# Keys', features' and q's float32 products moved to halves of TensorE's columns or rows

## The chip, the cores and the metric

One core of a Trainium2 chip runs one program. The metric is the device time of one execution in microseconds (us). TensorE is PE in the views, and its weight loads are PEld; VectorE is DVE, ScalarE is ACT, GpSimd is POOL, and SyncE (SP) issues the DMAs.

## What is computed

Linear attention with a product feature map, 4 batches, 4 heads, 1088 tokens, head width 32, r = 8, followed by a gated MLP (d_model 128, d_ff 1024) over the joined heads:

```python
def phi(x):
    a = np.einsum('rd,bhsd->bhsr', S1, x)
    b = np.einsum('rd,bhsd->bhsr', S2, x)
    return np.einsum('bhsi,bhsj->bhsij', a, b).reshape(*x.shape[:-1], r * r)
q_p, k_p = (phi(q), phi(k))
kv = np.einsum('bhsf,bhsd->bhfd', k_p, v)
z = np.sum(k_p, axis=2)
num = np.einsum('bhsf,bhfd->bhsd', q_p, kv)
den = np.einsum('bhsf,bhf->bhs', q_p, z)[..., None] + 1e-06
x = num / den                       # then [batch, seq, 128]
h = gelu(x @ w_in); u, v = halves of h
v_n = layernorm(v) * g_ln
v_s = np.einsum('ts,bsd->btd', w_sg, v_n) + b_sg[None, :, None]
out = x + (u * v_s) @ w_out
```

## The kernel before

Tokens are padded to 9 tiles of 128. Most of the work is the token-mixing product with `w_sg` (tiles `w_h`, `w_l` against the split features `ar`, PSUM tiles `pz`, lines 844 to 846). There, and in the products with `w_in` and `w_out`, a float32 number is split into a high and a low `float32r` word, and three matmuls (high x high, low x high, high x low) take the place of one float32 matmul.

Attention of a batch stands before that. For batches 1 to 3 it is written in `attention(b)`:

- **k step** (`k1`, L938): per token tile, one plain float32 matmul of the keys (128 columns of weights) with `sk` (128 moving columns, of which 64 are zero) gives both factors of the feature map. ACT copies one factor (L941), and DVE multiplies the two to 256 features (`features`, L260).
- **kv step** (`k2`, L951): per token tile, two float32 matmuls, one for each pair of heads; weights are 128 feature columns, 128 columns of v and ones move. Nine tiles add up in one PSUM tile.
- **q step** (`q2`, L975 to L980): per block `ci` of 364 tokens, q is split into two `float32r` words (ACT L969, DVE L970), and two matmuls (batches 2 and 3) or three (batch 1) of 364 columns give the factors. They go to DRAM (`dq`) and come back spread over partitions (`ea`, `eb`), are multiplied, split and used in `q3` (L1007 to L1009).

Batch 0 has its own code at the start: `k1_0` (L525), `k2_0` (L529), and `q2_0` (L603 to L605: 12 triples of 384 columns, from words that ACT and POOL make first). Before it, 14 small matmuls on a 64-column weight tile (L255) run; 12 more (`keep`, L707) stand where the main work is not ready yet.

Every step is a task with an engine; the list `ORDER` gives the sequence of all 1970 tasks, and each engine issues its own in that order. PSUM has three tiles `ps` for all steps of attention and of the MLP's inner products; a task that takes one waits until its last user has freed it.

Of the kernel before, what the change touches and what calls it, by code (L numbers as in the profile page):

```python
# [18 lines left out]
P = 128  # L19
NT = 9  # L20
# [125 lines left out]
class Plan:  # L146
# [9 lines left out]
    def add(self, eng, dur, f, r=(), w=(), take=(), free=(), pos=None, after=(), order=(), dma=(), port=0, tune=None):  # L156
# [13 lines left out]
        for k in r:  # L170
            if k not in w:
                self.read.setdefault(k, []).append(n)
        deps.discard(n)
        self.tasks.append(dict(eng=eng, dur=dur, f=f, deps=deps, take=take, free=list(free), pos=pos, order=set(order) - deps, dma=dma, port=port))
        return n

    def run(self):
# [1203 lines left out]
```

## Time and profile before

| | |
|---|---|
| median of 3 runs | 330.86 us (330.86 to 330.93) |
| span of the profiled execution | 328.9 us, so some 2.0 us of a run's time lie around the span |
| PE busy | 324.7 us, 99% of the span |
| DVE, ACT, POOL busy | 82%, 68%, 16% |
| chain that ended last | PE 99% |

The profiled execution has no time of its own beside its span; the 2.0 us are the median less the span. PE's records are durations from issue to a modelled end, and neighbours overlap. What one matmul costs in a full stream is the distance from one start to the next. A plain float32 matmul leaves two records.

### The profile page before, as it was taken

The numbers are of one execution on the slowest core, as the hardware profiler recorded it, in microseconds if no ns is written. First come the engines' busy times: TensorE is split into PE (matmuls) and PEld (weight loads), VectorE is DVE, ScalarE is ACT, GpSimd is POOL, SyncE is SP. The second block draws the span as 40 slices with busy tenths as digits, with TensorE's granted clock in tenths as the row PEclk, the third lists the DMA queues.
The fourth block names the chain that finished last, engine by engine and source line by source line (L and its number), as shares of the span: only waits on it lengthen the run. The fifth ranks groups of instructions, "written<-read, shape, count | busy, mean of one in ns | idle before, by whom it ended". The sixth has DMA issues, their size and how long they took to land.

```text
span 328.9 us, 5899 instructions
## 1 busy us (share of the span) xinstructions
PE 324.7 (99%) x1994; PEld 312.9 (95%) x1994; DVE 268.5 (82%) x595; ACT 223.3 (68%) x533; POOL 53.5 (16%) x130
## 2 busy tenths in 40 slices
PE   8999999999999999999999999999999999999996
PEld 8998899999999999999999999999999999999995
DVE  4799979999986899999883779897974587886755
ACT  6759994679899787457898776547889843522421
POOL 2696781000004200000013200000002200000000
PEclk9999999999999999999999999999999999999999
DMA  7999264675667777964675035932381029116702
GB/s 236 358 399 315 77 206 145 182 202 150 195 174 229 240 180 212 300 234 113 182 245 176 3 104 162 326 106 86 84 296 41 2 67 289 65 68 192 229 0 70
DMA packets 43854, 57.06 MB, mean 173 GB/s; under 512 B 4208, under 2 KB 41136, under 8 KB 43824
## 3 DMA queue, kind: packets, MB, share of 16 engines
q1 hardware_dynamic: 43680, 56.62, 54.8%
q8 instruction: 15, 0.25, 0.3%
q14 instruction: 15, 0.12, 0.1%
q10 hardware_dynamic: 144, 0.06, 0.1%
HBM read 46.73 MB, written 9.95 MB: 172 GB/s over the span
## 4 chain that ended last, share of the span: by engine, by line
PE 99%; DVE 0%; issue 0%; POOL 0%; POOLq 0%
PE pz L844 16%; PE pz L845 16%; PE pz L846 15%; PE ps L951 4%; PE ps L759 2%; PE ps L760 2%; PE po L798 2%; PE ps L761 2%; PE po L796 2%; PE po L797 2%; PE pz L855 2%; PE pz L856 2%; PE ps L938 2%; PE ps L1040 2%; PE ps L1041 2%; PE ps L1042 2%
## 5 line engine op out<-in xcount | busy, mean ns | idle before, releaser
L844 PE MATMUL pz<-w_h,ar 128*128 128x420 f32 (+1 forms) x288 | 94.4, 328 | 0.0
L845 PE MATMUL pz<-w_h,ar 128*128 128x420 f32 (+1 forms) x288 | 93.2, 324 | 0.0
L846 PE MATMUL pz<-w_l,ar 128*128 128x420 f32 (+1 forms) x288 | 93.1, 323 | 0.0
L844 PEld LDWEIGHTS pz<-w_h,ar 128*128 128x128 f32 x288 | 54.2, 188 | 1.9 <-DVE gt L775 0.4
L845 PEld LDWEIGHTS pz<-w_h,ar 128*128 128x128 f32 x288 | 54.1, 188 | 1.0
L846 PEld LDWEIGHTS pz<-w_l,ar 128*128 128x128 f32 x288 | 54.2, 188 | 0.6
L819 ACT CAST ar<-vn 128x512 fp32r<-128x512 f32 x40 | 24.5, 618 | 20.8 <-PE pz L846 19.9
L765 ACT ACTIVATE u<-ps 128x420 f32<-128x420 f32 (+1 forms) x48 | 22.4, 470 | 14.3 <-DVE gt L789 9.4
L790 ACT CAST gh<-gt 128x420 fp32r<-128x420 f32 (+1 forms) x47 | 23.0, 494 | 12.8 <-DVE gt L789 9.7
L820 DVE TENSOR_TENSOR ar<-vn,ar 128x512 fp32r<-128x512 f32 x40 | 27.2, 679 | 2.4 <-ACT ar L819 2.1
L323 ACT ACTIVATE vn<-vn,st 128x512 f32<-128x512 f32 x33 | 26.0, 811 | 1.4 <-POOL st L317 0.9
L791 DVE TENSOR_TENSOR gl<-gt,gh 128x420 fp32r<-128x420 f32 (+1 forms) x47 | 24.7, 531 | 1.6 <-ACT gh L790 1.2
L789 DVE TENSOR_TENSOR gt<-gt,u 128x420 f32<-128x420 f32 (+1 forms) x47 | 24.7, 532 | 0.5
L775 DVE SCALAR_TENSOR_TENSOR gt<-pz,g_col,b_bc 128x420 f32<-128x420 f32 (+1 forms) x31 | 17.8, 575 | 5.9 <-PE pz L856 3.8
L713 POOL TENSOR_TENSOR w_l<-w_f,w_h 128x420 fp32r<-128x420 f32 (+1 forms) x21 | 21.5, 1051 | 3.1 <-ACT w_h L666 2.7
L1052 ACT ACTIVATE kp<-vn,st 128x512 bf16<-128x512 f32 x27 | 19.4, 719 | 0.4
L1049 ACT ACTIVATE vn<-ps 128x512 f32<-128x512 f32 x27 | 16.0, 592 | 3.2 <-PE ps L1042 3.1
L306 POOL TENSOR_TENSOR st<-st 128x4 f32<-128x4 f32 (+2 forms) x8 | 2.2, 281 | 95.0 <-DVE st L288 95.0
L759 PE MATMUL ps<-x_h,win_h 128*128 128x420 f32 (+1 forms) x48 | 15.9, 332 | 0.0
L760 PE MATMUL ps<-x_h,win_l 128*128 128x420 f32 (+1 forms) x48 | 15.8, 329 | 0.0
L796 PE MATMUL po<-gh,wout_h 128*128 128x420 f32 (+1 forms) x47 | 15.7, 335 | 0.0
L761 PE MATMUL ps<-x_l,win_h 128*128 128x420 f32 (+1 forms) x48 | 15.7, 327 | 0.0
(311 smaller groups left out, 821.8 us busy)
## 6 DMA issues: line engine op xcount, KB each, us to landing
w_l<-td SPq DMA_DIRECT2D x52, 210.0 KB
w_h<-td SPq DMA_DIRECT2D x26, 420.0 KB
td<-tmp SPq DMA_DIRECT2D x16, 315.0 KB
w_f<-in_w SPq DMA_DIRECT2D x9, 544.0 KB
eb<-dq SPq DMA_DIRECT2D x12, 182.0 KB
ea<-dq SPq DMA_DIRECT2D x12, 182.0 KB
vn<-in_k SPq DMA_DIRECT2D x3, 576.0 KB
tmp<-in_w SPq DMA_DIRECT2D x16, 105.0 KB
```

Of the source, the lines that this page charges most:

```text
L323: A.activation(self.vn(t), self.vn(t), AF.Identity, bias=self.nm[:, t : t + 1], scale=self.rs[:, t : t + 1])
L759: mm(o, lhsT=win_h[:, ws], rhs=xh[:, cs], start=True, stop=False)
L760: mm(o, lhsT=win_l[:, ws], rhs=xh[:, cs], start=False, stop=False)
L765: add("A", 0.02 + ap(cw), lambda: A.activation(utt[plan.got[u]][:, :cw], ps(k)[:, :cw], AF.Gelu_apprx_tanh), r=[k], take={u: "u"}, free=[k ...
L789: add("V", dv(cw), lambda: V.tensor_mul(gt(k)[:, :cw], gt(k)[:, :cw], utt[plan.got[u]][:, :cw]), r=[u], w=[k], free=[u], port=1)
L790: add("A", ac(cw), lambda: A.copy(ght[plan.got[h]][:, :cw], gt(k)[:, :cw]), r=[k], take={h: "gh"})
L791: add("V", dv(cw), lambda: V.tensor_sub(glt[plan.got[l]][:, :cw], gt(k)[:, :cw], f32(ght[plan.got[h]][:, :cw])), r=[h, k], take={l: "gl"}, ...
L819: add("A", ac(n), lambda: A.copy(dst[:, 0], q()), r=r, w=[key])
L820: add("V", dv(n), lambda: V.tensor_sub(dst[:, 1], q(), f32(dst[:, 0])), r=r, w=[key], port=1)
L844: mm(o, lhsT=ar[e][:, 0, t], rhs=wh, start=first, stop=False, skip_group_check=True)
L845: mm(o, lhsT=ar[e][:, 1, t], rhs=wh, start=False, stop=False, skip_group_check=True)
L846: mm(o, lhsT=ar[e][:, 0, t], rhs=wl, start=False, stop=last, skip_group_check=True)
```

## The change

- k step: each token tile's 128 tokens are split in two halves of 64. Each half is a matmul with 64 columns of weights and 64 moving columns (`sk[:, :64]`); the first writes PSUM partitions 0 to 63, the second 64 to 127. In batches 2 and 3 three tiles make one task with one ACT copy; in batch 1 a task remains one tile.
- kv step: one matmul per head (64 weight columns, 64 moving columns), written to the two halves of the partitions in turn. In batches 2 and 3 all nine tiles are one task; the features now lie in `vn` instead of three turning `kp` tiles.
- q step: no split into words. Two plain float32 matmuls, each with the same 64 weight columns and one half (182 columns) of the block, on the two halves of the columns. The store to `dq` is two DMAs, the `eb` fill one DMA instead of two, the `ea` fill two as before.
- batch 0 likewise: `k1_0` 18 half products, `k2_0` 36, and `q2_0` 12 float32 products of 384 columns with 64 rows of weights each, in place of 36 `float32r` ones.
- The feature columns are ordered by head, the mask and `kv` are made to fit; the words `sk_h`, `sk_l`, `sk_w` and `qt` are gone. `ORDER` is new throughout; `free` now also waits for a tile's last readers when the list is made, and some helpers return their instruction. Nothing else changes.

```diff
-    step("skh", "A", 0.27, lambda: A.copy(sk_h, sk), ["sk"])
-    step("skl", "V", 0.25, lambda: V.tensor_sub(sk_l, sk, f32(sk_h)), ["skh"], w=["sk_l"], port=1)
...
     def k1_0(c):
-        for t in range(3 * c, 3 * c + 3):
-            mm(ps(("pk0", c))[:, P * (t % 3) : P * (t % 3) + P], lhsT=k0[:, P * t : P * t + P], rhs=sk, start=True, stop=True)
...
+        for i in range(6):
+            t, e = 3 * c + i // 2, i % 2
             mm(
+                ps(("pk0", c))[64 * e : 64 * e + 64, 64 * (i // 2) : 64 * (i // 2) + 64],
+                lhsT=k0[:, P * t + 64 * e : P * t + 64 * e + 64], rhs=sk[:, :64], start=True, stop=True,
+            )
+
+    def by_head(o, t, kp, v0, v1):
+        for h in range(H):
+            p, e, d = h // 2, 64 * (h % 2), D * (h % 2)
+            mm(
+                o[e : e + 64, 64 * p : 64 * p + 64], lhsT=kp[:, 64 * h : 64 * h + 64], rhs=(v1 if p else v0)[:, :, d : d + D],
                 start=(t == 0 and p == 0), stop=(t == NT - 1 and p == 1), skip_group_check=True,
             )
...
-    def q2_0(j, i):
-        o, s2 = pab0(j, i), [x[:, P * (2 * i + j % 2) :][:, :P] for x in sw]
-        h, l = qw[j // 2]
-        mm(o, lhsT=s2[0], rhs=h, start=True, stop=False)
-        mm(o, lhsT=s2[0], rhs=l, start=False, stop=False)
-        mm(o, lhsT=s2[1], rhs=h, start=False, stop=True)
+    def q2_0(c, i):
+        for p in range(2):
+            r = slice(64 * p, 64 * p + 64)
+            mm(pab0(2 * c + p, i), lhsT=sab()[r, i, p], rhs=q0[c][r], start=True, stop=True)
...
+        size = 1 if b == 1 else 3
+        for c in range(NT // size):
+            pk = ("pk", b, c)
+
+            def k1(c=c, pk=pk):
+                for i in range(2 * size):
+                    t, e = size * c + i // 2, i % 2
                     mm(
-                        ps(pkv)[:, P * p : P * p + P], lhsT=kpt(t % 3)[:, P * p : P * p + P],
-                        rhs=vh(1)[:, 0 : t + 2 : t + 1] if p else vh(0)[:, t : NT + 1 : NT - t],
-                        start=(t == 0 and p == 0), stop=(t == NT - 1 and p == 1), skip_group_check=True,
+                        ps(pk)[64 * e : 64 * e + 64, 64 * (i // 2) : 64 * (i // 2) + 64],
+                        lhsT=vn[:, t, 256 * s + 64 * e : 256 * s + 64 * e + 64], rhs=sk[:, :64], start=True, stop=True,
                     )
...
+        def k2(ts):
+            for t in ts:
+                by_head(ps(pkv), t, vn[:, t, 256 * s : 256 * s + 2 * P], vh(0)[:, t : NT + 1 : NT - t], vh(1)[:, 0 : t + 2 : t + 1])
+
+        for ts in [range(t, t + 1) for t in range(NT)] if b == 1 else [range(NT)]:
...
-            add("A", ac(cw), lambda cw=cw: A.copy(qtt[0][:, :cw], qld[:, :cw]), r=["qld"], w=["qh"])
...
+            def q2(hw=hw, pab=pab):
+                for e in range(2):
+                    mm(ps(pab)[64 * e : 64 * e + 64, :hw], lhsT=sk[:, 64:], rhs=qld[:, hw * e : hw * e + hw], start=True, stop=True)
...
+            add("A", ap(hw), lambda hw=hw, pab=pab: A.copy(abt[:, :hw], ps(pab)[:, :hw]), r=[pab], w=["ab"], free=[pab])
```

**PE at the start** (batch 0; L534 is `k1_0`, L611 `q2_0`, L542 `k2_0` of the change, L525, L603 to L605 and L529 those of before). Before:

```order
L525 MATMUL ps_118<-sk,k_99 128x128 x3
L525 MATMUL ps_119<-sk,k_99 128x128 x3
L529 MATMUL pz_121<-sg_vx,vn 128x128 x8
L603 MATMUL po_122<-ar_91,ar_93 128x384
L604 MATMUL po_122<-ar_92,ar_93 128x384
L605 MATMUL po_122<-ar_91,ar_94 128x384
```

The change:

```order
L534 MATMUL ps_113<-sk,k_95 64x64 x6
L611 MATMUL po_117<-r_97,sg_sab 128x384
L611 MATMUL pz_114<-r_97,sg_sab 128x384
L542 MATMUL pz_115<-sg_vx,vn 64x64 x36
L611 MATMUL ps_112<-r_97,sg_sab 128x384
```

The feature products of batch 0, spread over three stretches before, are one block of 36, with q's products ahead of it and behind it.

**PE in batch 1's k steps**, among the first token-mixing products (L695 and L697 of before are L703 and L705 of the change; L707 and L715 are `keep`). Before, with L938 a k step and L978 to L980 a q step:

```order
L707 MATMUL pz_120<-win_h 128x512 x7
L938 MATMUL ps_117<-sk,vn 128x128
L978 MATMUL ps_119<-qth,sk_h 128x364
L979 MATMUL ps_119<-qth,sk_l 128x364
L980 MATMUL ps_119<-qtl,sk_h 128x364
L938 MATMUL ps_118<-sk,vn 128x128
L695 MATMUL po_122<-w_h,ar_93 128x420
```

The change, with L950 a k step and L989 a q step:

```order
L705 MATMUL po_118<-w_h,ar_89 128x248
L715 MATMUL pz_114<-win_h 128x512
L950 MATMUL ps_113<-sk,vn 64x64 x2
L989 MATMUL ps_111<-qld,sk 64x182 x2
L950 MATMUL ps_112<-sk,vn 64x64 x2
L703 MATMUL po_116<-w_h,ar_89 128x420
L705 MATMUL po_116<-w_h,ar_89 128x420
L950 MATMUL ps_111<-sk,vn 64x64 x2
```

A pair of 64-column products stands alone between 128-column ones in several places.

**PE in batch 2's k and kv steps** (L844 to L846 before and L852 to L854 of the change are token mixing). Before:

```order
L938 MATMUL ps_118<-sk,vn 128x128
L796 MATMUL po_123<-gh_896,wout_h 128x420
L797 MATMUL po_123<-gh_896,wout_l 128x420
L798 MATMUL po_123<-gl_899,wout_h 128x420
L951 MATMUL ps_119<-ea,kp_107 128x128
L951 MATMUL ps_119<-eb,kp_107 128x128
```

The change:

```order
L950 MATMUL ps_112<-sk,vn 64x64 x6
L950 MATMUL ps_111<-sk,vn 64x64 x6
L989 MATMUL ps_113<-qld,sk 64x180 x2
L852 MATMUL pz_114<-w_h,ar_89 128x248
```

```order
L854 MATMUL pz_115<-w_l_393,ar_87 128x248
L542 MATMUL ps_112<-ea,vn 64x64 x2
L542 MATMUL ps_112<-eb,vn 64x64 x2
```

Six half products in a row take the place of three single tiles, and the kv step of the batch is one block of 36 half products (18 rows like the last two) ahead of which all nine tiles' features must be done.

## Rows read from the trace of the kernel before

**Rows 1.** The page: engines' busy time; chain that ended last, by engine.

```profile
PE 324.7 (99%) x1994; PEld 312.9 (95%) x1994; DVE 268.5 (82%) x595; ACT 223.3 (68%) x533; POOL 53.5 (16%) x130
...
PE 99%; DVE 0%; issue 0%; POOL 0%; POOLq 0%
```

**Rows 2.** Busy time by stretch: us, then each engine's, granted clock, DMA.

```profile
34.00:100.00 66.00, 65.97 (x398) 63.41 (x398) 61.91 (x134) 54.02 (x131) 15.00 (x32) 1.00 0.58 170
100.00:165.00 65.00, 65.00 (x404) 63.10 (x403) 58.42 (x128) 48.65 (x119) 6.31 (x24) 1.00 0.70 209
165.00:235.00 70.00, 69.97 (x438) 67.88 (x437) 56.54 (x118) 49.66 (x122) 6.41 (x22) 1.00 0.45 139
```

**Rows 3.** PE groups by form, line first: busy us, mean ns, idle before.

```profile
L951 PE MATMUL ps<-ea,kp 128*128 128x128 f32 x54 | 10.5, 275 | 0.0
L951 PE MATMUL ps<-eb,kp 128*128 128x128 f32 x54 | 10.4, 275 | 0.0
L938 PE MATMUL ps<-sk,vn 128*128 128x128 f32 x54 | 10.3, 279 | 0.0
```

**Rows 4.** PE timeline of batch 1's kv step: start us, length us.

```profile
37.81 0.39 PE L951 MATMUL ps<-ea,kp 128*128 128x128 f32 x2
38.03 0.39 PE L951 MATMUL ps<-eb,kp 128*128 128x128 f32 x2
38.25 0.39 PE L938 MATMUL ps<-sk,vn 128*128 128x128 f32 x2
```

**Rows 5.** PE timeline of the start.

```profile
1.01 3.25 PE L255 MATMUL ps<-kp 128*64 128x64 f32 x28 [1.01 <-POOL kp L253]
4.19 3.47 PE L525 MATMUL ps<-sk,k 128*128 128x128 f32 x18
...
12.36 0.33 PE L603 MATMUL po<-ar,ar 128*128 128x384 f32 x1
12.53 0.33 PE L604 MATMUL po<-ar,ar 128*128 128x384 f32 x1
...
20.26 2.79 PE L571 MATMUL pz<-sg_kvx,vn 128*128 128x66 f32 x24
22.86 0.48 PE L631 MATMUL ps<-win_h,x_h 128*128 128x512 f32 x1
```

**Rows 6.** Instructions of lines 255, 525 and 571: ns min/median/max.

```profile
L255 PE MATMUL ps<-kp x28: 313/314/368, 1.0 to 3.9; 128*64 128x64 f32 x28
...
L525 PEld LDWEIGHTS ps<-sk,k x18: 192/333/337, 4.2 to 7.3; 128*128 128x128 f32 x18
L525 PE MATMUL ps<-sk,k x18: 275/421/582, 4.2 to 7.4; 128*128 128x128 f32 x18
...
L571 PEld LDWEIGHTS pz<-sg_kvx,vn x36: 186/192/193, 15.5 to 22.7; 128*128 128x128 f32 x36
```

**Rows 7.** PEld timeline: the first two weight loads of L525 and L571.

```profile
4.19 0.50 PEld L525 LDWEIGHTS ps<-sk,k 128*128 128x128 f32 x2
...
15.52 0.30 PEld L571 LDWEIGHTS pz<-sg_kvx,vn 128*128 128x128 f32 x2 [0.34 <-DVE sg_kvx L541]
```

**Rows 8.** PE timeline of batch 2's first q step and its neighbours.

```profile
67.60 0.33 PE L975 MATMUL ps<-qth,sk_w 128*128 128x364 f32 x1
67.76 0.33 PE L976 MATMUL ps<-qtl,sk_w 128*128 128x364 f32 x1
67.93 0.35 PE L693 MATMUL po<-w_l,ar 128*128 128x420 f32 x1
```

**Rows 9.** DVE timeline of the start, around the low words of w_in.

```profile
11.59 0.43 DVE L460 TENSOR_SCALAR sp_wi_t<-sg_wraw_wi 128x512 int32<-128x512 int32 x1 [0.59 <-DMA sg_wraw_wi<-in_w_in]
...
20.80 1.50 DVE L483 TENSOR_TENSOR win_l<-sp_wi_t,sp_wi_e 128x512 fp32r<-128x512 f32 x1
22.23 0.54 DVE L626 TENSOR_TENSOR x_l<-ps,x_h 128x384 fp32r<-128x384 f32 x1
```

**Rows 10.** Instructions on tiles qt, ab and dq: ns min/median/max.

```profile
L970 DVE TENSOR_TENSOR qtl<-qld,qth x9: 474/527/1290, 33.9 to 188.6; 128x364 fp32r<-128x364 f32 x6, 128x360 fp32r<-128x360 f32 x3
...
L989 SPq DMA_DIRECT2D dq<-ab x9: 485/502/546, 36.5 to 202.6; - x9
...
L985 DVE TENSOR_TENSOR ab<-ps,ab x6: 480/518/529, 68.7 to 202.1; 64x364 f32<-64x364 f32 x4, 64x360 f32<-64x360 f32 x2
```

More of the change, by code (lines that the diff above doesn't have):

```diff
@@ L173, in add @@
         deps.discard(n)
-        self.tasks.append(dict(eng=eng, dur=dur, f=f, deps=deps, take=take, free=list(free), pos=pos, order=set(order) - deps, dma=dma, port=port))
+        order = set(order)
+        for k in free:
+            order.update([self.wrote[k]], self.read.get(k, ()))
+        order = order - deps - {n}
+        self.tasks.append(dict(eng=eng, dur=dur, f=f, deps=deps, take=take, free=list(free), pos=pos, order=order, dma=dma, port=port))
         return n
@@ L958, in attention @@
+        def k2(ts):
+            for t in ts:
+                by_head(ps(pkv), t, vn[:, t, 256 * s : 256 * s + 2 * P], vh(0)[:, t : NT + 1 : NT - t], vh(1)[:, 0 : t + 2 : t + 1])
+        for ts in [range(t, t + 1) for t in range(NT)] if b == 1 else [range(NT)]:
+            add("PE", 0.44 * len(ts), lambda ts=ts: k2(ts), r=[("vn", s, t, i) for t in ts for i in range(2)] + ["ea", "eb"], w=[pkv] if ts[0] else [],
+                take={} if ts[0] else {pkv: "ps"}, tune=at(b, "m", ts[0]))
         kv = kp0
@@ L990, in attention @@
+            for e in range(2):
+                load_(0.3, lambda hw=hw, ci=ci, e=e: load(
+                    dq[ci].rearrange("r p c -> (r p) c")[:, hw * e : hw * e + hw], abt[64 * e : 64 * e + 64, :hw]
+                ), r=["ab"], w=[("dq", ci, e)])
             for i, e in ((1, "ea"), (0, "eb")):
                 def fill(cw=cw, ci=ci, i=i, e=e):
-                    o = here(e)[:, :, :cw]
-                    if i:
-                        return tuple(load(o[:, p], dq[ci][32 + 16 * p : 48 + 16 * p, :cw].unsqueeze(0).broadcast_to([R, 16, cw])) for p in range(2))
@@ L995, in fill @@
-                    return tuple(load(o[:, p], dq[ci][16 * p : 16 * p + 16, :cw].unsqueeze(1).broadcast_to([16, R, cw])) for p in range(2))
-                add("SP", 1.2, fill, dma=(-1.55, -1.55) if i else (0.65, 0.65), r=[("dq", ci)], w=[e])
-            add("V", dv(2 * cw), port=1, f=lambda cw=cw: V.tensor_mul(now["ea"][:, :, :cw], now["ea"][:, :, :cw], now["eb"][:, :, :cw]), r=["eb"], w=["ea"])
-            add("A", ac(2 * cw), lambda cw=cw: A.copy(here("r0", F32R)[:, :, :cw], now["ea"][:, :, :cw]), r=["ea"], w=["r0"])
@@ L1000, in attention @@
-            add("V", dv(2 * cw), port=1, f=lambda cw=cw: V.tensor_sub(here("eb", F32R)[:, :, :cw], now["ea"][:, :, :cw], f32(now["r0"][:, :, :cw])), r=["ea", "r0"], w=["eb"])
+                    o = both_pairs(here(e), cw)
+                    src = dq[ci][16 * i : 16 * i + 16].rearrange("r p c -> r (p c)")
+                    if i == 0:
+                        return load(o, src.unsqueeze(1).broadcast_to([2 * R, R, 2 * cw]))
+                    src = src.rearrange("(h r) c -> h r c", h=2)
@@ new lines, in fill @@
+                    return tuple(
+                        load(o[64 * h : 64 * h + 64], src[h].unsqueeze(0).broadcast_to([R, R, 2 * cw])) for h in range(2)
+                    )
+                add("SP", 1.2, fill, dma=(-1.55, -1.55) if i else (0.65,), r=[("dq", ci, 0), ("dq", ci, 1)], w=[e])
+            add("V", dv(2 * cw), port=1, f=lambda cw=cw: V.tensor_mul(*(both_pairs(now[x], cw) for x in ("ea", "ea", "eb"))), r=["eb"], w=["ea"])
+            add("A", ac(2 * cw), lambda cw=cw: A.copy(both_pairs(here("r0", F32R), cw), both_pairs(now["ea"], cw)), r=["ea"], w=["r0"])
@@ L1001, in attention @@
+            add("V", dv(2 * cw), port=1, f=lambda cw=cw: V.tensor_sub(both_pairs(here("eb", F32R), cw), both_pairs(now["ea"], cw), f32(both_pairs(now["r0"], cw))), r=["ea", "r0"], w=["eb"])
             for p in range(2):
@@ L1005, in q3 @@
                     o, kv = ps(pd)[:, :cw], [kpt(i)[:, P * p : P * p + P] for i in (1, 2)]
[L1006 removed]
+                    qp = [both_pairs(now[n], cw)[:, cw * p : cw * p + cw] for n in ("r0", "eb")]
                     mm(o, lhsT=kv[0], rhs=qp[0], start=True, stop=False)
@@ L1225, in tile_kernel @@
     gates = {0: g}
-    dq = [dram.tile([64, CW], F32, name=f"dq{i}") for i in range(3)]
+    dq = [dram.tile([32, 2, cw], F32, name=f"dq{i}") for i, (c0, cw) in enumerate(CA)]
     def at(b, kind, i):
@@ L1244, in new_swaps @@
         G.memset(now["r2"][:, 360:], 1.0)
-    swapped = [add("G", 0.1, new_swaps, w=[("r", 2, 0), ("r", 2, 1)], after=[ids["pk0", c] for c in range(3)] + [ids["ql", c] for c in range(3)] + [ids["tr", c] for c in range(2)])]
+    swapped = [add("G", 0.1, new_swaps, w=[("r", 2, 0), ("r", 2, 1)], after=[ids["pk0", c] for c in range(3)] + [ids["q2_0", c, i] for c in range(3) for i in range(2)] + [ids["tr", c] for c in range(2)])]
     unit(0, (1, 0))
@@ L1361 @@
     wd[0:64, NT - 1] = wd[64:128, NT - 1] = wt[P * (NT - 1) :]
-    own = np.kron(np.tile(np.eye(2, dtype=np.float32), (R, 1)), np.ones((R, D), np.float32))
+    own = np.kron(np.eye(2, dtype=np.float32), np.ones((R * R, D), np.float32))
     arrays = dict(
```

148 lines of the change are left out of this document (57 added, 91 removed), and 178 rows, old and new, of the table ORDER.

## The prediction

> **What bounds the kernel now.** First the page: PE is busy in 99% of the span and the chain that ended last is PE to 99% [rows 1]. So the question is what PE does, not who makes it wait. Busy time of PE says little by itself, since neighbouring records overlap; but the chain has no other engine in it, and by stretch PE has no gap either: 65.97 of 66, 65.00 of 65, 69.97 of 70 us [rows 2]. A change here pays what it takes out of PE's stream or puts into it, as long as the others keep up. DVE is the one that might not: 61.91 of 66 us in the stretch of batch 1's attention, 58.42 of 65 and 56.54 of 70 after it [rows 2].
>
> Next, what the touched products cost in the stream. The kv step has 54 + 54 records for 54 products, the k step 54 for 27: a plain float32 product leaves two records [rows 3]. In batch 1 three neighbours start at 37.81, 38.03 and 38.25 us, so a product of 128 weight columns and 128 moving columns takes 0.22 us, 0.112 a record, though each record lasts 0.275 [rows 3, 4]. With only 66 moving columns it is no cheaper: 24 records in 2.79 us, less the last one's 0.275, are 0.109 each [rows 5]. So it is the 128 weight columns that set this pace: two successive weight loads start 0.30 - 0.19 = 0.11 us apart [rows 6, 7]. That is the slack the change goes for: half the array's columns need half the load, and zeros or other heads' values no longer move through.
>
> **What 64 columns cost.** One row shows it: 28 matmuls with 64 weight columns and 64 moving ones take 3.25 us, less the last one's 0.314, 0.109 each [rows 5, 6]. This is at the start, and the k step's records just behind, of one and the same form, last 0.421 us in the median and 0.275 at least [rows 6]: TensorE begins at the lower of its two levels (1.2 GHz), and rises to 2.4 within those 18 records, after the small matmuls and ten of the 18 have run. In the stretches of batches 1 to 3 the granted clock is 1.00, the upper level [rows 2], so there I halve the 0.109: 0.055 a record, 0.11 for a half product of two records. All 28 lie on the same columns of the array, so the row gives the price of half products **one after another**: two of them cost what one full product costs now, 0.22 us. Whether two on different halves run **side by side** no row of before shows. That is the unknown on which the result turns; its ends are 0.055 a record (no overlap) and half of it.
>
> **The sum, part by part**, for batches 1 to 3.
>
> - k and kv steps. Before: 27 + 54 products x 0.224 = 18.1 us. After: 54 + 108 half products, 18.1 us one after another, 9.1 if all are paired. The code alternates the halves product by product, and a product's two records are on the same half, so in a run of n half products the second record of one can lie beside the first of the next: n + 1 places instead of 2n. The kv blocks are runs of 28 and 8 (batch 1), 36 and 36: 38 + 37 + 37 = 112 places. The k steps come in runs of 2 to 18, about 62 places. 174 x 0.056 = 9.7 us: **-8.4 us**.
> - q step. Before, a matmul of 364 columns takes 0.166 us (67.60, 67.76, 67.93) [rows 8]; three for each block of batch 1 and two in batches 2 and 3, 21 in all: 3.5 us. After, a block is two float32 products of 182 columns, two records each; 182 columns twice through the array are a 364-column record, 0.166. One after another 36 x 0.166 = 6.0 us; by the same pairing three places a block, 27 x 0.166 = 4.5; fully paired 3.0. I take 4.5: **+1.0 us**. Here PE pays for what ACT and DVE are spared.
> - Changes of shape. Now 128-column and 64-column products alternate in PE's stream. From the order, batches 1 to 3 have 15 stretches of half products between full ones, so 30 changes. The trace has one such change, from L255 to L525 at 4.19 us: the first two weight loads span 0.50 us, less 0.337 for the second, so they start 0.163 apart, where after an idle gap without a change it is 0.30 - 0.192 = 0.108 [rows 6, 7]. So a change costs at least 0.055 us. The last small matmul ends at 1.01 + 3.25 = 4.26, after the 4.19 [rows 5]: the load may well have waited for that end, and the gap ahead of it then hid part of the wait. In a full stream the end lies 0.275 - 0.112 = 0.163 us behind the next start [rows 3, 4], and the new weights (0.055 or 0.108) can't be loaded ahead: up to 0.22 into a stretch and 0.27 out of it. 30 changes are 1.7 to 7.4 us. I take 0.12 each, above the one measured, which had a gap to hide in: **+3.6 us**.
>
> The Trainium skill, "TensorEngine Tiling (Array Packing)", section "Key Properties", says that tiles of different columns load and multiply in parallel, but that a change of the tiling mode drains TensorE. The row agrees that the change costs something; that tiles run in parallel no run here shows yet. By a full drain the sum is the dear end above.
>
> - The start (batch 0). `k1_0`, `k2_0` and `q2_0` cost now some 3.3 us (4.19 to 7.50), 4.0 (36 records x 0.112) and 6.3 (36 x 0.17, from starts 12.36 and 12.53 [rows 5]). Paired they would be about 2.3, 2.1 and 5.3: 4 us less on PE. I count little of it. The first product with `w_in`, at 22.86 us, comes right after DVE wrote `x_l` (22.23 + 0.54), and that stood on DVE behind `win_l`, which ends at 22.30 [rows 5, 9]. DVE has been on that chain since `w_in` landed at 11.59; the change takes only the small `sk_l` off it and keeps all feature products and q products. If PE is through earlier there, it waits, and `keep` matmuls fill in. **-0.5 us**, between -2 and +2 (one after another, `q2_0` would be 24 records of 2 x 0.17 = 8.2).
> - At nothing: ACT's two or three small copies and casts fewer per step, DVE's 9 `ql` (0.527 each) and 6 sums into `ab` (0.518) [rows 10]. They lie beside a full PE. Their loss is what keeps DVE below PE if PE gets shorter: some 7.9 us less DVE over the three batches against 7.4 less PE. SP issues as many DMAs for a block as before, six (a second store, one `eb` fill less), at 0.5 us [rows 10]; the store of the second half is queued behind the first, 0.5 us later, and the fills behind it. In the order q3 still stands behind many groups of token mixing after its q step, so I let nothing wait for that.
>
> Sum: -8.4 + 1.0 + 3.6 - 0.5 = -4.3 us. The profiled execution has 328.9 us of span and, by the median, 2.0 around it; the sum is made against that 330.9, which is the median shown: **326.5 us**.
>
> **The rivals.**
>
> 1. *Forecast: halves run side by side.* For it: within the array, a weight load already runs beside a product [rows 6, 7], so two things at once are nothing new to it; and the rows at 66 columns show that half the streaming capacity lies idle. Its own range: changes of shape at 0.055, all paired and the start at -2 give -9.1 - 0.5 + 1.7 - 2 = -9.9, 321; changes at 0.245 give -8.4 + 1.0 + 7.4 - 0.5 = -0.5, 330.4. 64%.
> 2. *Weight loads stay one after another,* and only products overlap. For it: a load of 128 columns sets the pace now, and 64 + 64 columns are as much to load. Then the k and kv steps gain nothing, q costs +1.0, the changes +3.6: 330.9 + 4.6 = 335.5, **slower**. It decides as soon as two loads on different halves start no closer than 0.055 us. 16%.
> 3. *Nothing overlaps.* k and kv nothing, q +2.5, changes +3.6, `q2_0` at the start +2: 339. 10%. This is also the case in which the change does not do what its name says.
> 4. *PE is faster, and the others are not.* In batches 2 and 3 the kv block needs all nine tiles' features (0.42 us each on DVE) before its first record, in batch 1 DVE is at 94% [rows 2]. Then the 4 us come back as waits for `vn` or `ps`: 330.5. The order puts some ten groups of three other matmuls between the last k step of batches 2 and 3 and the kv block, which speaks against it. 8%.
> 5. *Load and product exclude each other on halves:* each record is 0.055 + 0.055. k and kv go to 324 x 0.11 = 35.6 us, +17.5, q and changes on top: 352. The Trainium skill, "TensorE: Matmul & The Clock Gate", Part 3, says that a weight load overlaps with running matmuls only where the row groups differ, and halves of columns share their rows; in the trace of before they overlap with the same rows, at 0.112 a record for a load of 0.108 and a product. 2%.
>
> **How the numbers follow.** A measurement of this kernel can tell about 0.2% (0.7 us) from no change. Of the forecast's 64%, changes at the dear end leave 3 in the middle and 2 slower; of the fourth rival's 8, 4 are faster, 3 the same, 1 slower; rivals 2, 3 and 5 are slower. Faster 0.63, same 0.06, slower 0.31. The range goes from 320.5 (one in twenty lies below) up to 337, past the second rival and short of the third, so that some 15% are left out above and below. The forecast's own range is 321 to 330.4.
>
> **What would show it.** Right: records of 64-column products starting some 0.03 us apart on average, with pairs of starts close together; a kv block of 36 half products in about 2.1 us; q blocks in about 0.5 us; PE still at 99%. Rivals 2 and 3: the kv block at 4 us, records 0.055 apart. The changes of shape show as the distance from the last full matmul's expected end to the first half product's start, and back. The fourth: idle time on PE ahead of kv blocks or q3, ended by DVE or a DMA. The prediction is wrong if the pairing holds and the time still rises, or if the start moves by more than 2 us.

## The result, and the profile after

The changed kernel takes 335.44 us (median of 4 runs, 333.52 to 337.15), the kernel before 330.89 beside it: a ratio of 1.0125, 95% interval 1.0078 to 1.0171. (Medians here and below are over all runs; ratios and intervals leave out runs in a slower state of the chip, so the two can differ by up to 1%.) It is slower by about 1.25%, where 326.5 us and a gain were forecast. The profiled execution took 333.52 us with a span of 331.7.

The page of the changed kernel, its busy times and the chain that ended last, against [rows 1]:

```profile
PE 317.7 (96%) x2213; PEld 294.7 (89%) x2213; DVE 265.5 (80%) x579; ACT 215.0 (65%) x506; POOL 48.2 (15%) x125
...
PE 64%; DVE 14%; ACT 7%; DMA 6%; issue 4%; POOL 3%; SPq 1%; DVEq 0%; ACTq 0%; POOLq 0%
```

TensorE is busy 7.0 us less, but is no longer the whole chain: 64% instead of 99%. By stretch (us, then each engine's busy time, granted clock, DMA), against [rows 2]:

```profile
34.00:100.00 66.00, 62.91 (x441) 55.79 (x441) 59.12 (x126) 47.13 (x122) 14.76 (x34) 1.00 0.66 182
100.00:165.00 65.00, 65.00 (x468) 61.45 (x467) 56.03 (x120) 45.51 (x106) 4.90 (x24) 1.00 0.60 184
165.00:235.00 70.00, 69.28 (x506) 66.37 (x506) 56.86 (x120) 50.47 (x124) 5.90 (x22) 1.00 0.54 161
```

In batches 2 and 3 TensorE is nearly as full as before (65.00 of 65 and 69.28 of 70 us). In batch 1's stretch it stands for 3 of 66 us. The first 40 us, which the rows ahead of the prediction left out, in the kernel before:

```profile
10.00:20.00 10.00, 9.97 (x70) 9.54 (x69) 9.12 (x23) 8.44 (x14) 7.27 (x8) 1.00 1.00 388
20.00:30.00 10.00, 10.00 (x64) 8.72 (x64) 9.24 (x29) 5.83 (x11) 6.94 (x9) 1.00 1.06 368
30.00:40.00 10.00, 9.97 (x61) 8.45 (x60) 9.67 (x30) 9.49 (x31) 8.50 (x20) 1.00 0.41 133
```

and in the changed kernel:

```profile
10.00:20.00 10.00, 9.23 (x85) 6.78 (x81) 7.53 (x21) 7.28 (x12) 4.65 (x5) 1.00 1.00 397
20.00:30.00 10.00, 7.95 (x38) 5.65 (x37) 9.15 (x22) 7.36 (x10) 7.86 (x10) 1.00 0.76 258
30.00:40.00 10.00, 8.62 (x63) 5.98 (x63) 9.55 (x32) 8.04 (x29) 6.36 (x20) 1.00 0.65 204
```

Before, the transfers were full as well up to 30 us (a share of 1.00 and 1.06) and VectorE worked 9.1 to 9.7 of 10 us. Neither VectorE nor the transfers had room to follow a faster TensorE, and after the change TensorE waits. What it waits for, from the list of waits of the changed kernel (total us, times, longest):

```profile
PE ps L641 <- DVE x_l L634: 1.5, 2, 1.1
PE ps L640 <- DVE win_l L497: 1.4, 1, 1.4
PE ps L1020 <- DVE eb L1011: 1.4, 1, 1.4
PE ps L950 <- ACT ab L992: 1.1, 2, 0.7
PE ps L534 <- DMA k<-in_k: 1.0, 1, 1.0
```

Another count, used below: starts of matmuls that come more than 0.2 us later than the median distance behind a matmul of that line and shape. These delays sum to 15.2 us, 12.3 of them before 72 us; in the kernel before they are 0.4 us.

**The halves do what was forecast.** The kv block of batch 2 in the timeline of PE (start us, length us), against [rows 4]:

```profile
110.44 0.28 PE L853 MATMUL pz<-w_h,ar 128*128 128x248 f32 x1
110.56 0.28 PE L854 MATMUL pz<-w_l,ar 128*128 128x248 f32 x1
110.77 0.34 PE L542 MATMUL ps<-ea,vn 128*64 128x64 f32 x4
110.93 0.29 PE L542 MATMUL ps<-eb,vn 128*64 128x64 f32 x4
111.05 0.29 PE L542 MATMUL ps<-ea,vn 128*64 128x64 f32 x4
...
112.80 0.29 PE L542 MATMUL ps<-eb,vn 128*64 128x64 f32 x4
113.01 0.38 PE L852 MATMUL pz<-w_h,ar 128*128 128x248 f32 x1
113.23 0.27 PE L853 MATMUL pz<-w_h,ar 128*128 128x248 f32 x1
```

Four records (two half products) start every 0.117 us, 0.029 a record: two halves run fully side by side. A run confirms it: in `u_apart` (below), with all left halves ahead of all right ones, the same block's starts span 4.01 us (from 112.93) instead of 2.10, 0.056 a record. The changes of shape stand in the same rows. Into the stretch: 0.21 instead of 0.12 us from L854 to the first half, and 0.16 instead of 0.117 to the next four. Out of it: 0.21 instead of 0.117, then 0.22 instead of 0.12. Together 0.33 us a stretch.

### The profile page after: what moved, and what is told of

It reads as the page before. It is cut to its first block, busy times and chain, and to the rows that moved or that the text cites. A ratio compares the mean times of both kernels' runs of the same rounds, so it can differ in the third digit from the quotient of the medians.

```text
span 331.7 us, 6268 instructions
## 1 busy us (share of the span) xinstructions
PE 317.7 (96%) x2213; PEld 294.7 (89%) x2213; DVE 265.5 (80%) x579; ACT 215.0 (65%) x506; POOL 48.2 (15%) x125
## 4 chain that ended last, share of the span: by engine, by line
PE 64%; DVE 14%; ACT 7%; DMA 6%; issue 4%; POOL 3%; SPq 1%; DVEq 0%; ACTq 0%; POOLq 0%
PE pz L852 14%; PE pz L853 13%; PE pz L854 13%; DMA w_f<-in_w 3%; PE po L804 2%; PE po L806 2%; PE po L805 2%; PE ps L767 2%; PE ps L768 2%; PE ps L769 2%; PE pz L863 2%; PE pz L864 2%; DMA r<-in_q 1%; PE ps L542 1%; PE ps L1051 1%
## 5 line engine op out<-in xcount | busy, mean ns | idle before, releaser
L852 PE MATMUL pz<-w_h,ar 128*128 128x420 f32 (+1 forms) x288 | 94.1, 327 | 0.0
L854 PE MATMUL pz<-w_l,ar 128*128 128x420 f32 (+1 forms) x288 | 93.1, 323 | 0.0
L852 PEld LDWEIGHTS pz<-w_h,ar 128*128 128x128 f32 x288 | 54.1, 188 | 2.7 <-DVE gt L783 0.8
L854 PEld LDWEIGHTS pz<-w_l,ar 128*128 128x128 f32 x288 | 54.1, 188 | 0.6
L827 ACT CAST ar<-vn 128x512 fp32r<-128x512 f32 x40 | 24.6, 617 | 14.2 <-PE pz L854 11.9
L721 POOL TENSOR_TENSOR w_l<-w_f,w_h 128x420 fp32r<-128x420 f32 (+1 forms) x21 | 21.4, 1048 | 17.3 <-ACT w_h L674 13.3
```

The source lines that it names most:

```text
L827: add("A", ac(n), lambda: A.copy(dst[:, 0], q()), r=r, w=[key])
L852: mm(o, lhsT=ar[e][:, 0, t], rhs=wh, start=first, stop=False, skip_group_check=True)
L854: mm(o, lhsT=ar[e][:, 0, t], rhs=wl, start=False, stop=last, skip_group_check=True)
```

## The experiments

The theory to test: halves are cheap, and time is lost because TensorE waits. Its rivals: **A**, the new list keeps TensorE hungry and another would not; **B**, the other engines' chains set the time before 72 us whatever the list; **C**, the granted clock falls in the waits. Each run was timed beside the kernel before on the same chip; its ratio is to that, while medians of different kernels can be from different chips.

**Lists moved freely** (`r_search`, `r_start`, `r_rest`, and `b_search` as the control on the kernel before): only numbers in `ORDER` change, 1331, 298, 995 and 1374 tasks out of place. Such an edit reads like this row, of `a_move1` below:

```diff
-    52, 48, 49, 50, 69, 47, 10, 46, 53, 54, 61, 57, 59, 55, 45, 62, 51, 70, 67, 78,
+    52, 48, 49, 50, 47, 10, 46, 53, 54, 61, 57, 59, 69, 55, 45, 62, 51, 70, 67, 78,
```

> The arithmetic of the changed kernel, only the list ORDER is another: the same tasks, moved so that TensorE's waits are filled, using durations read from the trace of the changed kernel. That trace has 15.2 us of TensorE's starts that came over 0.2 us late, 12.3 of them in the first 72 us, where the kernel before has 0.4 in all. Theory A (halves are as cheap as forecast, the list does not keep TensorE fed): about 10 us below the changed kernel, 323 to 327, so some 1 to 2.5 per cent below the kernel before. Theory B (the start and batch 1's attention are bounded by VectorE, ScalarE and the transfers themselves): no more than 2 us below the changed kernel, 332 to 336. Theory C (what is lost is TensorE's clock): also 332 to 336.

> As r_search, but only the list's first 440 tasks (to some 70 us of the span) are moved; the rest of the list is the changed kernel's. Theory A with the loss at the start: 7 of the 12.3 us of waits before 72 us go, 326 to 329. Theory B: within 2 us of the changed kernel, 332 to 336. If the loss came from the list after 70 us: no change, 333 to 336.

> As r_search, but only what stands behind the first 440 tasks is moved (from some 70 us on). Theory A with the loss at the start: only the 2.9 us of waits behind 72 us can go, 331 to 333. If the list after 70 us were what costs the time: 326 to 329. Theory B: 332 to 336.

> The control: the kernel before with its own arithmetic, its list moved in the same way with the durations of its own trace. Its TensorE waits over 0.2 us are 0.4 us in all, so theory A expects at most 2 us: 329 to 331. If a better list were worth 10 us to any arithmetic, it would come to 321 to 325, and the halves would have no part in what r_search gains.

Measured: 352.47 us (1.0531, 1.0475 to 1.0588), 342.25 (1.0306, 1.0263 to 1.0350), 343.69 (1.0333, 1.0284 to 1.0383), and the control 364.55 (1.0968, 1.0931 to 1.1005). All four missed, the control by most. Adding up durations along a list does not see which buffers a transfer waits for, and free moves use up slack that the sum doesn't see. They say nothing for A or B; they say that a list alone is worth 30 us and that two lists can't be compared as if only the arithmetic differed. One thing can be read: `r_start` cut the late starts before 30 us from 8.4 to 2.4 us, and between 30 and 62 us they rose from 3.3 to 10.1.

**The old list, few moves, halves apart.** `x_old`: the change's arithmetic, each task where its counterpart stood before. `a_move1` and `x_move1`: 61 and 75 tasks out of place (the texts below give other counts) by a rule that keeps slack. `u_apart`:

```diff
-                for i in range(2 * size):
+                for i in [*range(0, 2 * size, 2), *range(1, 2 * size, 2)]:
...
-            for t in ts:
-                by_head(ps(pkv), t, vn[:, t, 256 * s : 256 * s + 2 * P], vh(0)[:, t : NT + 1 : NT - t], vh(1)[:, 0 : t + 2 : t + 1])
+            for t, hs in [(t, hs) for hs in ((0, 2), (1, 3)) for t in ts]:
+                by_head(ps(pkv), t, vn[:, t, 256 * s : 256 * s + 2 * P], vh(0)[:, t : NT + 1 : NT - t], vh(1)[:, 0 : t + 2 : t + 1], hs)
```

> The changed kernel's arithmetic in the order of the kernel before: each of its 1899 tasks stands where its counterpart stood in the list before (a group of three k steps at the place of its first, the kv products of batches 2 and 3 at the place of their last), and only what its own dependences forbid is put later. This is the change that the prediction's sum was made for. Theory A (the loss is the new list's): 324 to 329, as the forecast had it. Theory B (the other engines' chains bound the start and batch 1's attention whatever the list, so that TensorE's 16.7 us come back as waits): 331 to 338, with over 10 us of TensorE waits again and most of them before 72 us.

> The changed kernel with 76 tasks of TensorE, VectorE and ScalarE moved in its list, each only where the move takes at least 0.02 us off a sum along the list in which the other engines' work is up to 12 per cent longer and a transfer up to 1.2 us later; tasks of GpSimd and SyncE and the w_h casts keep their places, and nothing moves for free. Theory A: the lists of the first four runs failed because their moves used up slack that the sum did not see, and this one is 3 to 6 us below the changed kernel, 328 to 331. Theory B: no gain, 333 to 338.

> x_old with 56 tasks moved under the same rule as a_move1. Theory A: 322 to 328, below the kernel before. Theory B: within 2 us of x_old and above 331.

> The changed kernel and its list, but the half products of a k or kv block stand with all left halves first and then all right ones, so that in the blocks of three tokens and in the kv blocks of batches 2 and 3 no left one runs beside a right one. Alone a record takes 0.056 us where a pair takes 0.058, so TensorE works 8 to 12 us longer in all (54 products in each of four batches at 0.054, less where neighbours still pair up). If TensorE sets the time everywhere: 341 to 346. If the waits before 72 us take up what batches 0 and 1 add and only batches 2 and 3 show: 337 to 341. If halves never ran side by side, or it does not matter: 333 to 337.

Measured: `x_old` 339.39 us (1.0231, 1.0198 to 1.0264), `a_move1` 331.38 (0.9993, 0.9966 to 1.0021), `x_move1` 337.45 (1.0121, 1.0071 to 1.0172), `u_apart` 339.23 (1.0233, 1.0188 to 1.0278). `x_old` has the change's arithmetic without its list, and it is 7.4 us slower than the kernel before: theory A in its simple form falls, and B had less in mind (331 to 338). It is not quite the kernel that the sum was made for, as its text has it: the sum counted the new list's 15 stretches of halves in batches 1 to 3, and `x_old`'s trace has 24, nine more at 0.33 us. But 61 moves bring the new list to the time of the kernel before, at the upper end of what A expected, so B isn't the whole either. `x_move1` came out as B had it.

`u_apart` costs 3.7 us over the changed kernel (335.49, below), but not of the 8 to 12 us of its text: TensorE's work did not grow by so much. In its trace the kv blocks of batches 2 and 3 span 4.01 and 4.22 us instead of 2.10 and 2.31, and their k groups grow by 0.1 to 0.2 each. Batch 0's kv block still pairs up (72 records in 2.15 us), and batch 1's stretches grow by 0.1 us in all. So some 4 us were added, all of them behind 90 us, and most of that shows in the time. About batches 0 and 1 this run says nothing. Its trace is 1.3 us late from the start for another reason. Batch 0's k step (L534) and q products (L611), in the changed kernel:

```profile
5.14 1.27 PE L534 MATMUL ps<-sk,k 128*64 128x64 f32 x36 [0.98 <-DMA k<-in_k]
6.34 0.59 PE L611 MATMUL po<-r,sg_sab 64*128 64x384 f32 x1
```

and in `u_apart`:

```profile
5.34 2.42 PE L534 MATMUL ps<-sk,k 128*64 128x64 f32 x36 [1.17 <-DMA k<-in_k]
7.69 1.01 PE L611 MATMUL po<-r,sg_sab 64*128 64x384 f32 x1
```

The q products are the same in both kernels and take nearly twice as long here: TensorE still ran at the lower of its two levels (1.2 GHz) in this execution. The trace's first entry of the granted clock, 1.00, is at 9.06 us, in the changed kernel's at 4.54. In the table below, about 1 us of a row can be this.

**VectorE doubled, and halves in batches 2 and 3 alone.** `a_again` is the changed kernel once more. `d_twice`:

```diff
-        return V.tensor_tensor(
+        return [V.tensor_tensor(
...
-        )
+        ) for _ in range(2)][-1]
```

`h_plain` is the kernel before with k and kv products by halves for `b > 1` only, in its own list; the features go to `vn` as in the change, and a second copy of `sk`'s columns in the order of heads is kept where the zeros were; `h_move1` has 30 tasks moved. Its core:

```diff
-                mm(ps(pk)[:, :P], lhsT=vn[:, t, 256 * s : 256 * s + P], rhs=sk, start=True, stop=True)
+                    for i in range(6):
+                        t, e = 3 * c + i // 2, i % 2
+                        mm(
+                            ps(pk)[64 * e : 64 * e + 64, 64 * (i // 2) : 64 * (i // 2) + 64],
+                            lhsT=vn[:, t, 256 * s + 64 * e : 256 * s + 64 * e + 64], rhs=sk[:, 64:], start=True, stop=True,
+                        )
```

> The changed kernel as it is, once more, beside the other three: 333 to 337, as in its four runs; it is what d_twice is compared with on the same chip.

> The changed kernel with each features product of VectorE written twice (36 instructions of 0.415 us, 3.7 us of VectorE more in each batch, the result the same). Theory B (before 72 us the chain runs over the other engines, so their work sets the time; behind it TensorE does): the first main products after 40 us come 4 to 7 us later than in the changed kernel, batches 2 and 3 add less than 1 us, 338 to 343 in all. Theory A (TensorE sets the time everywhere and only the list keeps it hungry): less than 2 us more, 334 to 338.

> The kernel before with halves for keys and features in batches 2 and 3 alone; batches 0 and 1 and q's products in all batches stay as they were, and 30 tasks of these batches are moved by the rule of a_move1. TensorE's work falls by 5.8 us (54 products of 0.112 saved by pairing and 18 places of nothing, twice) less four stretches at 0.33. Theory B (halves pay where TensorE sets the time, that is in batches 2 and 3, and not before 72 us): 326 to 329, faster than both kernels. If the saving comes back as waits there too: 330 to 333.

> As h_move1 without moved tasks: each task where its counterpart stood in the list before, a group of three k steps at the place of its first and the kv products at the place of their last. Against h_move1 it tells what the moved tasks are worth. Theory B: 327 to 331, at most 2 us behind h_move1. If what x_old lost came from its groups and kv blocks in the old order and not from the start: 333 to 338.

Measured: `a_again` 335.49 us (1.0115, 1.0084 to 1.0146), `d_twice` 347.40 (1.0448, 1.0403 to 1.0492), `h_move1` **328.80** (0.9913, 0.9890 to 0.9936), `h_plain` 329.07 (0.9910, 0.9891 to 0.9929). Where in the span the time goes is seen from products that no kernel changes (token mixing, gates, `w_in`, `w_out`): the first column counts how many us of such products were issued before (each at its median distance to the next), the others give the start of the next one in each trace.

```
us of them  before   after  u_apart  d_twice  h_move1   h_q0    x_q    x_old
     8       37.11   40.22   41.51    50.32    37.16    37.49   37.55   38.75
    24       59.33   60.68   61.94    73.97    59.25    59.23   59.76   60.96
    40       78.14   82.35   83.64    93.90    78.01    77.97   84.19   85.68
    90      137.75  141.03  145.12   153.22   137.03   139.46  146.05  147.75
   200      260.09  262.10  268.27   276.41   257.37   260.90  268.62  270.15
```

`d_twice` adds 3.7 us of VectorE in each batch. In the first two, where 7.5 us are added, it costs 13.3 by the row of 24 (73.97 - 60.68), more than B's 4 to 7; it is 11.6 at the row of 40 and 14.3 at the row of 200 (276.41 - 262.10), so the other two batches cost 1 to 3 more. By medians it is 11.9 in all, the changed kernel's trace being that of its fastest run. Part of the 13.3 may be the clock's and was not taken apart: from 16 to 20, 40 to 44 and 56 to 60 us `d_twice` was granted 0.67, 0.68 and 0.57, the changed kernel 1.00. `u_apart`, which adds TensorE work behind 90 us alone, loses 4.9 us there (6.2 at the row of 200 less the 1.3 of the start). So before some 62 us VectorE's chain sets the time, and in batches 2 and 3 TensorE's work does; that a saving of TensorE is worth nothing in batch 0 is tested by `h_0`, below. `h_move1` fits: halves where TensorE sets the time, and it is faster than both kernels. Its page is TensorE's again:

```profile
PE 321.1 (98%) x2102; PEld 307.0 (94%) x2102; DVE 268.1 (82%) x597; ACT 221.9 (68%) x521; POOL 54.3 (17%) x132
...
PE 81%; DVE 6%; DMA 5%; ACT 5%; issue 1%; SPq 1%; DVEq 0%
```

**Which part of the change costs.** The same code with the set of batches as a constant (a batch by halves has its features in the order of heads, so its `ea` fill is four DMAs instead of two): `h_0` (batch 0), `h_1` (batch 1), `h_0123` (all four, q still split), and `h_q0`, which is `h_0123` with batch 0's q taken as whole float32:

```diff
-        mm(o, lhsT=s2[0], rhs=h, start=True, stop=False)
-        mm(o, lhsT=s2[0], rhs=l, start=False, stop=False)
-        mm(o, lhsT=s2[1], rhs=h, start=False, stop=True)
+        r = slice(64 * (j % 2), 64 * (j % 2) + 64)
+        mm(pab0(j, i), lhsT=sab()[r, i, j % 2], rhs=q0[j // 2][r], start=True, stop=True)
```

> The kernel before with halves for keys and features in batch 0 alone, its list unchanged to the last number, q's products as they were. TensorE saves 2.9 us there (54 products at 0.054) less two or three stretches at 0.33. Theory B (the other engines set the time of the start): no gain, within 1 us of the kernel before, 331 to 334. If TensorE set it: 2 us less, 329 to 331. If halves in batch 0 are what costs the changed kernel its time: 334 to 338.

> The same for batch 1 alone, list unchanged but for the places of its 36 tasks in the numbering. Nine stretches of halves at 0.33 take back the 2.9 us they save, so TensorE's work there is as before: 331 to 334. If halves in batch 1 (a wait at each shape change, VectorE's features later) are what costs the changed kernel its time: 334 to 338.

> Halves for keys and features in all four batches, q's products and splits as in the kernel before, list as in h_plain. Beside x_old (the whole change in the same list, 339.4) it leaves out only q's part. If q's part is innocent: 336 to 340, as x_old. If the parts add up and keys and features cost nothing in batches 0 and 1: 328 to 331, and then some 9 us of x_old are q's, whose whole float32 products put its factors, the transfers that spread them and VectorE's products at other times.

> h_0123 with batch 0's q taken as whole float32 from 64 rows of sab (12 products, one for each half of the heads and each factor, at the places of the three-part products before), so ScalarE's four casts and GpSimd's four subtractions for them are gone; batches 1 to 3 keep their split q. x_old differs from it in two things: it writes two tiles with each of six merged q steps of batch 0, and it takes q of batches 1 to 3 as whole float32 halves with other transfers. If batch 0's float32 q costs the time by itself: 333 to 338. If it is the merged steps or the later batches' q: 327 to 331, and x_old's other 9 us lie in those two.

Measured: `h_0` 331.49 us (0.9986, 0.9968 to 1.0004), `h_1` 331.50 (0.9982, 0.9967 to 0.9998), `h_0123` 329.52 (0.9931, 0.9908 to 0.9955), `h_q0` 331.99 (0.9997, 0.9966 to 1.0027). Halves for keys and features gain nothing to speak of in batches 0 and 1, and cost nothing either; in batch 0 some 2 us less of TensorE are worth 0.4. `h_q0` lies between its two expectations. `x_old`, the same list with q's part as well, stands 9.9 us above `h_0123`.

**q, in both lists.** `x_q` is `x_old` with batch 0's merged q steps taken apart as in `h_q0`. `a_q` is the changed kernel's list with `h_q0`'s arithmetic. Their diffs are those of `h_q0` and the list.

> x_old (the whole change in the list of before, 339.4) with batch 0's six merged q steps taken apart into twelve at their old places, as in h_q0 (332.0); from h_q0 it then differs only in q of batches 1 to 3. If the merged steps cost what x_old loses: 332 to 334. If q of batches 1 to 3 (whole float32 halves, their products laid out for both pairs, two transfers out and three back for one and four) does: 336 to 339. In the traces the merged steps cost x_old 1.7 us by 24 us of main work and the rest came behind it, so the second is the likelier.

> The changed kernel's list with h_q0's arithmetic: q of batches 1 to 3 split and spread as in the kernel before (a cast and a subtraction ahead of each q step, a sum behind it in batches 2 and 3), batch 0's q steps apart but at the merged steps' places. Beside a_again (335.5) it takes q of batches 1 to 3 out of the change within the new list. If that q is what costs the changed kernel its time: 330 to 333. If the list's start is: 334 to 338, since the waits on win_l and x_l before 40 us stay.

Measured: `x_q` 339.71 us (1.0206, 1.0162 to 1.0250), `a_q` 340.00 (1.0250, 1.0226 to 1.0275). In the list of before, q of batches 1 to 3 costs 7.7 us (331.99 to 339.71; 6.9 by the two ratios), and the merged steps nothing. `a_q` missed both expectations: with the q it was not made for, the new list is 4.5 us slower than with its own.

By the table most of the 7.7 us of `x_q` are lost at one place: behind `h_q0` by 0.5 us at 24, by 6.2 at 40. It is batch 1's attention. SyncE's DMA issues there in the kernel before (start us, length us):

```profile
45.22 0.41 SPq L968 DMA_DIRECT2D qld<-in_q  x1
45.68 0.42 SPq L894 DMA_DIRECT2D tmp<-in_w  x1
46.16 0.42 SPq L881 DMA_DIRECT2D td<-w_h  x1
49.07 1.22 SPq L995 DMA_DIRECT2D eb<-dq  x2
50.38 1.30 SPq L994 DMA_DIRECT2D ea<-dq  x2
54.99 0.34 SPq L894 DMA_DIRECT2D tmp<-in_w  x1
```

and in `x_q` (its lines are numbered 3 lower than the changed kernel's; 981 loads `qld`, 999 and 1002 spread q's factors, 899 loads a weight tile):

```profile
45.16 0.37 SPq L897 DMA_DIRECT2D tmp<-in_w  x1
51.80 0.35 SPq L981 DMA_DIRECT2D qld<-in_q  x1
52.19 0.43 SPq L899 DMA_DIRECT2D tmp<-in_w  x1
...
53.20 0.58 SPq L999 DMA_DIRECT2D eb<-dq  x1
53.83 2.04 SPq L1002 DMA_DIRECT2D ea<-dq  x2
55.91 0.45 SPq L899 DMA_DIRECT2D tmp<-in_w  x1
```

The load of the third block of q goes out at 51.80 instead of 45.22, and behind it every other. The list of SyncE's waits of `x_q` from 30 to 75 us says why:

```profile
SPq L981 <- PE ps L986: 7.8, 2, 6.2
```

`qld` is one buffer. Before, ScalarE's cast and VectorE's subtraction read the second block from it, the latter until 44.06 us, and TensorE came to that block's q step at 50.85. Now TensorE itself reads it, at 51.2 us in this list, and SyncE, which issues in order, stands for 6.2 us with the weight loads and the spreads behind. The weight load that VectorE needs next goes out at 55.91 us instead of 54.99, now right behind the spreads; it lands 6.8 us later, where VectorE used it at 57.61 before. VectorE has its own order, and meets the late weight tile first:

```profile
56.23 0.41 DVE L971 TENSOR_TENSOR kp<-ps,mask 128x256 f32<-128x256 f32 x1
62.82 0.38 DVE L905 SCALAR_TENSOR_TENSOR tmp<-tmp 128x210 f32<-128x210 f32 x1 [6.19 <-DMA tmp<-in_w]
63.30 0.82 DVE L909 TENSOR_TENSOR tmp<-tmp 128x630 fp32r<-128x630 f32 x1
64.03 0.91 DVE L1006 TENSOR_TENSOR ea<-ea,eb 128x728 f32<-128x728 f32 x1
```

The last row is q's product, which the kernel before starts at 58.81 us; TensorE's q3 waits behind it:

```profile
65.83 0.44 PE L1015 MATMUL ps<-r,kp 128*128 128x364 f32 x1 [1.75 <-ACT r L1007]
66.56 0.43 PE L1016 MATMUL ps<-r,kp 128*128 128x364 f32 x1 [0.29 <-DVE kp L976]
67.99 0.67 PE L1017 MATMUL ps<-eb,kp 128*128 128x364 f32 x1 [0.99 <-DVE eb L1008]
```

Of the 5.7 us lost between the rows of 24 and 40, late starts from L1015 on are 4.0. The rest lies with the clock (0.61 granted from 68 to 72 us, behind the wait) and with q blocks that now stand alone between full products (61.60 and 73.45 us), each with its two changes of shape; five more of these stand behind 84 us, at 0.33 about the 1.5 us that `x_q` still loses there. That the early-emptied buffer is the cause of the wait is read from this trace; a kernel with a second `qld`, or with the copy kept, was not run.

The changed kernel's own list answers to this: its second q step of batch 1 runs at 42.2 us instead of 51, and the loads and spreads go out accordingly (SyncE's issues of the changed kernel, among others):

```profile
42.70 0.35 SPq L984 DMA_DIRECT2D qld<-in_q  x1
...
48.18 1.39 SPq L1005 DMA_DIRECT2D ea<-dq  x2
49.67 0.55 SPq L1002 DMA_DIRECT2D eb<-dq  x1
```

SyncE waits only 0.9 us for TensorE's read of `qld` there. The changed kernel stands 3.1 us behind at the row of 8 all the same, after its waits for `win_l` and `x_l`, and 4.2 at the row of 40: its q3 products of batch 1 start 0.6 and 1.6 us late (61.62 and 63.63 us), the second on VectorE's `eb`. Whether one paid for the other was not tried. By medians: 331.9 before, 329.5 with k and kv halves everywhere, 332.0 with batch 0's float32 q, 339.7 with the other batches' q, 339.4 with the merged steps, and 335.5 with the new list, which gives back 3.9.

## Why the prediction was wrong

- *TensorE bounds the kernel, and a change pays what it takes out of its stream.* Read rightly from [rows 1, 2] for the kernel as it stood, and wrong as a price: 99% of one engine doesn't say how far the next is behind. Shown by `d_twice` and `h_0`: before 62 us the price is VectorE's.
- *Halves run side by side.* Right: 0.029 us a record, and the kv block's 36 half products in 2.1 us, as the text asked. Rivals 2, 3 and 5 fall. The Trainium skill, "TensorEngine Tiling (Array Packing)", section "Key Properties", has both rules that matter here, tiles of different columns in parallel and a drain at a change of mode; the rows above agree with the first (0.029 us a record) and with a cost of the second (0.33 us a stretch). The rule that rival 5 quotes from the Trainium skill, "TensorE: Matmul & The Clock Gate", Part 3, does not hold here as quoted: halves on the same rows start every 0.029 us, not every 0.11, so their loads overlapped. The same Part also names a load into the background weight buffer as one that goes ahead of running matmuls; no run here shows which case this is.
- *q step, +1.0 us on TensorE.* Too dear: a block's two halves run side by side, some 0.32 us a block and 2.9 in all, as in the text's fully paired case, so it is -0.6.
- *Changes of shape, 0.12 us each.* Mis-sized: 0.33 a stretch, 0.167 a change. The 15 stretches of batches 1 to 3 cost 5.0 us, not 3.6.
- *k and kv steps, -8.4 us for batches 1 to 3.* Right where TensorE sets the time: `h_plain` takes batches 2 and 3 alone and gains 3.3 us; its sum is 2 x 54 x (0.112 - 0.058) = 5.8 saved less 8 stretches at 0.33, 3.2. In batch 1 nine stretches take the saving back, and nothing is left (`h_1`).
- *"At nothing": ACT's, DVE's and SP's part of q, which "lie beside a full PE", and "I let nothing wait for that".* **This is the step that failed.** Before 72 us PE isn't full once its work shrinks: the changed kernel's late starts there are 12.3 us (0 before), nearly all on other engines and transfers, and by the table it stands 4.2 us behind at the row of 40, of which batches 2 and 3 give 2 back. In the list of before the same arithmetic shows one such wait plainly. The sum counted what the split costs to compute and not what it did to a buffer: it emptied `qld` early. Without it the next load stands on SyncE until TensorE has read, with everything behind it. Q of batches 1 to 3 is worth 7.7 us in that list, 5.7 of them around this one place (6.2 less 0.5). The store that was looked at, 0.5 us, was the wrong instruction of the same queue. In the changed kernel's own list this wait is 0.9 us, and the loss stands at the start and at batch 1's q3, on VectorE; which of the list's moves brought it there stays open.
- *The start, -0.5 us between -2 and +2.* The reason given was right (VectorE's chain to `x_l` is not shortened: `win_l` ends at 22.62 us, 21.54 + 1.08, before at 22.30), and the bound was not: with the new list the row of 8 stands at +3.1. With the old list and the same arithmetic but for the merged steps it is +0.4 (`x_q`), and the new list with q split is as late (`a_q`, 41.06, +3.9), so this part is the list's. The prediction had named a start that moves by more than 2 us, and a rise of the time with the pairing intact, as signs of being wrong; both came.
- *Rival 4, the others are not faster, at 8% and 330.5 us.* Right in kind, and priced as a gain lost; it can do more than cancel a gain, since a wait on an in-order queue is passed on to all that stands behind.

C has a share: `a_again`'s six runs go from 334.21 to 337.88 us at granted clocks of 0.986 to 0.994, while `h_move1`'s stand at 0.997 to 1.000. It is not the whole: the changed kernel's two runs at a granted clock of 1.000 took 333.52 and 334.67 us, still 2.6 and 3.8 above the kernel before, and those at 0.994 and 0.988 took 336.20 and 337.15. A profiled run with a stretch at the lower level, below, is 0.7 us longer than one without.

The sum's terms give 326.6 us, 330.9 - 4.3, and not 326.5.

Left open: why `h_q0` is 2.5 us behind `h_0123`, although it is not behind the kernel before down to the row of 40 (in its trace batch 2's kv block starts 1.0 us late at 113.21, behind features for which VectorE first stood 0.9 and 0.4 us for weight tiles, and batch 3's first k step 0.9 late at 181.26, on the load of its keys; why these land later was not traced), and which moves of the new list cost the start. That a list which beats `h_move1` exists with all of q's part wasn't shown: the best one tried, `a_move1`, equals the kernel before.

## What to carry to other kernels

Where one engine is at 99%, price a saving by the engine that is next, stretch by stretch: double a piece of that engine's work and a piece of the first one's, and see which the time follows. Read from the trace how much work was really added: `u_apart` added some 4 of the 8 to 12 us that its text counted on, and in two batches only. Before removing a copy, cast or split, ask which buffer it empties, and who loads into that buffer next on an in-order queue. And where a list is tuned by hand or search, test arithmetic in the unchanged list, part by part; the gain here was to be had in two of four batches (`h_move1`, 0.9% faster than before).

## What the hardware showed unexpectedly

- Two half products on different column halves overlap completely, weight loads included: the four records of such a pair take 0.117 us in the rows of 110.93 to 112.80, though each has a weight load of 0.138 us of its own, where a full product's two records take 0.224.
- The granted clock falls behind waits of TensorE. In `a_again`, by stretch:

```profile
20.00:24.00 4.00, 1.86 (x10) 1.20 (x10) 3.90 (x8) 3.10 (x3) 3.22 (x4) 1.00 1.00 370
24.00:28.00 4.00, 4.00 (x13) 3.21 (x12) 3.54 (x8) 2.32 (x4) 4.00 (x6) 0.60 0.50 96
```

TensorE had worked 1.86 of 4 us, and then runs at 0.60, much of the stretch at the lower level (1.2 GHz). The span is 332.4 us, against 331.7 where this stretch was at 1.00: most of what is lost there was a wait anyway.
